# Packed attention and a GELU feed-forward on one core: a new table of priorities for the kernel's planner, with other lengths of the first transfers and a smaller margin on landings

## The chip, the core and the metric

The kernel runs on one core of a Trainium2 chip. The core has five engines with an instruction queue of their own: PE (TensorE, matrix products), ACT (ScalarE), DVE (VectorE), POOL (GpSimd) and SP (SyncE), which here only issues transfers (DMAs) between the chip's main memory and the core's memory. Each engine works its queue off in order and waits on semaphores for the others. The metric is the device time of one execution in microseconds (us), given as the median of several runs.

## The reference: what is computed

```
s  = softmax(p @ k^T / 8) @ v            # p: 32 packed queries a head; k, v: 576 x 64
a  = softmax(q @ s^T / 8) @ s            # q: 576 x 64; 8 batches x 8 heads
x  = a, heads side by side               # 4608 x 512
h  = x @ w_in                            # 512 x 2048
g  = 0.5 * h * (1 + erf(h / sqrt(2)))
out = g @ w_out                          # 2048 x 512, float32
```

## The kernel before, in words

The program is unrolled: Python code walks through all of the work once and emits one instruction stream for each engine. Batches are taken in pairs (four pairs, `NP`), and the hidden width of 2048 in four blocks of 512 (`NF`), which gives 16 units `u` of 8 steps. A step is one tile h (L1140 and L1149 on PE, with the packed product s @ w_in as a weight, `wp`, made by L1045 or L1084), then gelu on ACT (L1172), a rounded copy on ACT (L1179) and the rest by subtraction on DVE (L1181), which together are g, and then 12 matmuls of g with w_out (L1202 to L1204, name o). A pair's remainder of 64 rows a batch goes through POOL (L1192, L1193) and the o_edge matmuls. The two attention products of the first pair stand in the head of the program, in chunks of four heads: load, transposes on PE (L468 for k and q, L515 for p), scores (L591, L543), softmax on ACT and DVE, transposes of the weights (L667), the product with v (L707) and its transpose (L722). For the later pairs they are mixed into the steps of the pair before. The weights arrive as 64-bit words and are decoded (L980, L981 on ACT, L987 to L993 on DVE, L1007 to L1021 on POOL), kept in main memory once (L1026) and loaded again in later pairs (L948).

What stands where in each engine's queue is decided by a planner inside the kernel, the class `Order`. It holds a clock of its own, gives each operation an engine, a cost and a priority (`step`; the smallest goes first), and issues an operation as soon as its inputs, its buffers and its engine are free by that clock. The chip doesn't follow the clock, only the order that comes out of it. Four things in it matter here.

- Priorities come from the tables `FIRST` (the first pair), `SECOND` and `LATER` (the others), `LEAD` (weights), and `PATIENCE` and `STEADY` (how much later an operation may be and still go ahead of one that doesn't suit the engine at the moment).
- A transfer lands by the clock after an issue time, the bytes of its cost over 390 KB a microsecond, and a latency. For all that are issued after 1.5 us (`DMA_EARLY`) a margin `DMA_SLACK` is put on top.
- Where PE has nothing that is ready by the clock, and the first output matmul hasn't been issued, the planner emits a **filler**, a matmul on a constant tile `still` (L1122), of 0.11 us by its clock. In the profile and the order a PSUM tile that fillers used keeps the name idle, so `idle<-still` are the fillers, and `idle<-ident,k` is a transpose that took such a tile.
- Up to eight transfers are under way by the clock; SP issues them all.

```
done = self.under_way[-1] + (DMA_SLACK if self.now > DMA_EARLY else 0.0)
...
if engine == PE and self.idle and self.idle():
    self.free[PE] = self.now + self.clock(self.now, IDLE, True)
```

## Time and profile before

| | before |
|---|---|
| median of 3 runs | 729.41 us (729.28 to 729.71) |
| the profiled execution | 729.62 us |
| its span, first to last instruction | 727.8 us |
| matmuls on PE | 5594, of which 202 are fillers |
| moved by DMA | 106.8 MB |

Times in the profile are microseconds from the span's start. A row of a group gives the line, the engine, the operation with its output and inputs, how often it stands there, its busy time with the mean of one in ns, and the idle time of the engine before it with what ended it. A row of a timeline gives start, duration, line and operation, and in brackets the idle time before it. Matmuls overlap: PE's place is read from the distance of starts, not from the duration of one. A row of the DMA view gives the transfer, its size and the time from issue to landing.

### The profile page before, as it was taken

The numbers are of one execution on the slowest core, as the hardware profiler recorded it, in microseconds if no ns is written. First come the engines' busy times: TensorE is split into PE (matmuls) and PEld (weight loads), VectorE is DVE, ScalarE is ACT, GpSimd is POOL, SyncE is SP. The second block draws the span as 40 slices with busy tenths as digits, with TensorE's granted clock in tenths as the row PEclk, the third lists the DMA queues.
The fourth block names the chain that finished last, engine by engine and source line by source line (L and its number), as shares of the span: only waits on it lengthen the run. The fifth ranks groups of instructions, "written<-read, shape, count | busy, mean of one in ns | idle before, by whom it ended". The sixth has DMA issues, their size and how long they took to land.

```text
span 727.8 us, 13835 instructions
## 1 busy us (share of the span) xinstructions
PE 722.8 (99%) x5594; PEld 595.3 (82%) x5594; DVE 395.1 (54%) x608; ACT 347.3 (48%) x591; POOL 157.5 (22%) x331
## 2 busy tenths in 40 slices
PE   9999999999999999999999999999999999999998
PEld 7777787787878887887788887877887888888887
DVE  5898767888488334334687332444578321424322
ACT  4667775686365533553263343626254243324221
POOL 2554564644310100010111101101011101111110
PEclk9999999999999999999999999999999999999999
DMA  9959669697537967084723968053833603020122
GB/s 331 402 196 178 213 219 192 208 236 194 181 88 128 206 177 149 1 214 92 171 76 117 202 149 204 11 181 57 133 116 116 217 30 145 30 91 26 41 75 73
DMA packets 155135, 106.80 MB, mean 147 GB/s; under 512 B 123200, under 2 KB 129600, under 8 KB 155072
## 3 DMA queue, kind: packets, MB, share of 16 engines
q1 hardware_dynamic: 155072, 105.93, 56.1%
q8 instruction: 44, 0.72, 0.4%
q14 instruction: 19, 0.16, 0.1%
HBM read 83.89 MB, written 22.02 MB: 146 GB/s over the span
## 4 chain that ended last, share of the span: by engine, by line
PE 99%; ACT 0%; DVE 0%; issue 0%; ACTq 0%
PE h L1149 27%; PE o L1202 17%; PE o L1204 16%; PE o L1203 16%; PE wps L1084 4%; PE idle L1122 3%; PE s L543 2%; PE o_edge L1202 2%; PE o_edge L1204 2%; PE o_edge L1203 2%; PE pp L707 1%; PE h L1140 1%; PE e1Tm L655 1%; PE idle L707 1%; PE km L468 1%; PE qm L468 0%
## 5 line engine op out<-in xcount | busy, mean ns | idle before, releaser
L1149 PEld LDWEIGHTS h<-a2T,wp 128*128 128x128 f32 x1488 | 207.7, 188 | 9.0 <-ACT graw L1172 1.0
L1149 PE MATMUL h<-a2T,wp 128*128 128x288 f32 x1488 | 214.3, 295 | 0.6 <-ACT graw L1172 0.6
L1181 DVE TENSOR_TENSOR g<-graw,g 128x512 fp32r<-128x512 f32 x128 | 92.9, 726 | 208.5 <-ACT g L1179 198.7
L1172 ACT ACTIVATE graw<-h 128x576 f32<-128x576 f32 x127 | 82.3, 652 | 257.7 <-PE h L1149 201.6
L1202 PE MATMUL o<-w,g 128*128 128x512 f32 x508 | 204.8, 403 | 0.0
L1204 PE MATMUL o<-w,g 128*128 128x512 f32 x508 | 198.9, 392 | 0.0
L1203 PE MATMUL o<-w,g 128*128 128x512 f32 x508 | 198.8, 391 | 0.0
L1192 POOL CAST t<-graw 128x64 fp32r<-128x64 f32 x128 | 38.1, 298 | 495.2 <-ACT graw L1172 447.2
L1202 PEld LDWEIGHTS o<-w,g 128*128 128x128 f32 x508 | 95.4, 188 | 35.2 <-issue 16.8
L1204 PEld LDWEIGHTS o<-w,g 128*128 128x128 f32 x508 | 95.3, 188 | 21.5
L1203 PEld LDWEIGHTS o<-w,g 128*128 128x128 f32 x508 | 95.5, 188 | 15.4
L1179 ACT CAST g<-graw 128x512 fp32r<-128x512 f32 x128 | 79.6, 622 | 9.0 <-PE o L1204 6.4
L1288 DVE TENSOR_TENSOR acc<-o,acc 128x512 f32<-128x512 f32 x96 | 64.0, 685 | 33.6 <-PE o L1204 33.5
L1193 POOL TENSOR_TENSOR t<-graw,t 128x64 fp32r<-128x64 f32 x128 | 45.7, 357 | 10.2
L1096 DVE TENSOR_TENSOR wp<-wps,wp 128x1024 fp32r<-128x1024 f32 x30 | 35.3, 1218 | 13.7 <-ACT wp L1095 13.6
L1095 ACT CAST wp<-wps 128x1024 fp32r<-128x1024 f32 x30 | 29.0, 1018 | 15.2 <-PE wps L1084 15.2
L1084 PE MATMUL wps<-w,pp 64*32 64x512 f32 x480 | 29.2, 595 | 0.0
L1122 PE MATMUL idle<-still 128*128 128x256 bf16 x202 | 27.7, 286 | 1.1 <-DVE still L396 1.1
L993 DVE SCALAR_TENSOR_TENSOR wt<-wraw,wt 128x512 int32<-128x512 int32 x32 | 26.1, 814 | 0.6
L1015 POOL TENSOR_TENSOR wt<-wt 128x512 int32<-128x512 int32 x16 | 21.3, 1332 | 21.5 <-DVE wt L993 15.9
L1202 PE MATMUL o_edge<-w,t 128*128 128x512 f32 (+1 forms) x68 | 25.8, 379 | 0.0
L1122 PEld LDWEIGHTS <-still 128*128 128x128 bf16 x202 | 19.8, 102 | 7.3 <-issue 3.3
(138 smaller groups left out, 670.1 us busy)
## 6 DMA issues: line engine op xcount, KB each, us to landing
w<-ws SPq DMA_DIRECT2D x72, 512.0 KB, 5.2
ws<-w SPq DMA_DIRECT2D x24, 512.0 KB, 3.6
wraw<-in_moe_w_in_dram SPq DMA_DIRECT2D x16, 512.0 KB, 5.1
wraw<-in_moe_w_out_dram SPq DMA_DIRECT2D x16, 512.0 KB, 4.4
k<-in_k_dram SPq DMA_DIRECT2D x48, 144.0 KB, 4.8
q<-in_q_dram SPq DMA_DIRECT2D x48, 144.0 KB, 5.5
out_dram<-acc SPq DMA_DIRECT2D x26, 256.0 KB, 2.1
v<-in_v_dram SPq DMA_DIRECT2D x12, 512.0 KB, 4.4
```

The lines of the kernel that those rows point to most:

```text
L1084: nc.tensor.matmul(t[r0:r0 + 32, hh], lhsT=pp[b][rows, hh, r0:r0 + 32], rhs=wi[u, hh][rows, g], start=True, stop=True)
L1122: nc.tensor.matmul(bank(t)[:, :256], lhsT=still[:, :P], rhs=still, start=True, stop=True)
L1149: nc.tensor.matmul(t[:, half, :HALF], lhsT=w[:, wpart, ch, fc], rhs=a2T[b, ch][:, apart, half * HALF:(half + 1) * HALF], start=ch == 0 and ...
L1172: lambda raw: nc.scalar.activation(raw.rearrange("p (a n) -> p a n", a=2), t[:, :, :HALF], AF.Gelu),
L1179: g = yield Op(ACT, 0.52, lead, lambda g: nc.scalar.copy(g[:, 0], main), [(gts, f"g_{n}")])
L1181: DVE, 0.6, lead, lambda: nc.vector.tensor_tensor(g[:, 1], main, g[:, 0].bitcast(F32), ALU.subtract),
L1192: nc.gpsimd.tensor_copy(dst[:, 0], side)
L1193: nc.gpsimd.tensor_tensor(dst[:, 1], side, dst[:, 0].bitcast(F32), ALU.subtract)
L1202: nc.tensor.matmul(t, lhsT=g[0], rhs=w[:, 0], start=first, stop=False)
L1203: nc.tensor.matmul(t, lhsT=g[0], rhs=w[:, 1], start=False, stop=False)
L1204: nc.tensor.matmul(t, lhsT=g[1], rhs=w[:, 0], start=False, stop=last)
L1288: yield Op(DVE, 0.6, n, lambda: nc.vector.tensor_tensor(a, x, a, ALU.add))
```

## The change

Only numbers are changed. The margin on landings, `DMA_SLACK`, goes from 2.0 to 0.8 us. The sizes from which the planner works out the length of the first pair's transfers and of the weights' are smaller. And all entries of the tables of priorities are new; among them one chunk instead of two has its softmax subtraction and multiplication on POOL (`gpsimd`), the four copies of the first packed products are all on ACT (`copy`), one chunk's scores use another PSUM ring (`banks`), and one set of k's transposes is evacuated by ACT instead of DVE (`turn`).

```diff
-DMA_SLACK, DMA_EARLY = 2.0, 1.5
+DMA_SLACK, DMA_EARLY = 0.8, 1.5
...
-    "p": (-549.25, -438.34),
-    "k": (-613.55, -468.03, -440.86, -350.31),
+    "p": (-1320.01, -453.87),
+    "k": (-1227.69, -1055.77, -668.22, -531.18),
...
-    "gpsimd": (1, 2),
-    "copy": ("DVE", "ACT", "DVE", "ACT"),
-    "banks": (True, True, False, True),
-    "turn": {"k": ("ACT", "DVE", "DVE", "DVE"), "q": ("DVE", "ACT", "ACT", "ACT")},
+    "gpsimd": (1,),
+    "copy": ("ACT", "ACT", "ACT", "ACT"),
+    "banks": (True, True, True, False),
+    "turn": {"k": ("ACT", "DVE", "ACT", "DVE"), "q": ("DVE", "ACT", "ACT", "ACT")},
...
-        cost, fn = ((4, 1800e3, 1.1), blocks) if bt.b >= 2 else ((1, 650e3), ninths) if name == "k" else ((1, 620e3), rows)
+        cost, fn = ((4, 1800e3, 1.1), blocks) if bt.b >= 2 else ((1, 575e3), ninths) if name == "k" else ((1, 570e3), rows)
...
-        cost, fn = ((1, 650e3), ninths) if s.b < 2 else ((2, 900e3, 0.6), fn)
+        cost, fn = ((1, 610e3), ninths) if s.b < 2 else ((2, 900e3, 0.6), fn)
...
-        raw = yield Op(DMA, (1, 590e3 if i < 2 else 530e3), load_step, fetch, [(raws, f"wraw_{n}")])
+        raw = yield Op(DMA, (1, 530e3 if i < 2 else 510e3), load_step, fetch, [(raws, f"wraw_{n}")])
```

What it does to the queues is shown at three places. First SP's queue at the start of the program (names carry the batch and the chunk, then a number of the buffer). Before:

```order
L429 DMA k_0_0_84<-in_k_dram 128x2x576
L974 DMA wraw_0_0_1_86<-in_moe_w_in_dram 128x2x512
L509 DMA p_0_90<-in_p_dram 128x2x64 x2
L974 DMA wraw_0_1_0_97<-in_moe_w_in_dram 128x2x512
L970 DMA wraw_0_2_0_101<-in_moe_w_out_dram 128x1024
L429 DMA k_0_1_106<-in_k_dram 128x2x576
L426 DMA q_0_0_110<-in_q_dram 128x1152
```

and now:

```order
L509 DMA p_0_84<-in_p_dram 128x2x64 x2
L970 DMA wraw_0_2_0_89<-in_moe_w_out_dram 128x1024
L429 DMA k_0_0_93<-in_k_dram 128x2x576
L429 DMA k_0_1_97<-in_k_dram 128x2x576
L974 DMA wraw_0_0_1_101<-in_moe_w_in_dram 128x2x512
L429 DMA k_1_0_106<-in_k_dram 128x2x576
L974 DMA wraw_0_1_0_110<-in_moe_w_in_dram 128x2x512
```

p is now first, k third and fourth with a weight of w_out ahead of them, and q, which was seventh, comes fourteenth.

Second, PE's queue up to the first transposes of k. Before, 18 fillers stand ahead of these rows, 16 behind:

```order
L1122 LDWEIGHTS still_72
L1122 MATMUL idle_88<-still_72 128x256
L468 MATMUL idle_88<-ident_71,k_0_0_84 128x128 x3
L468 MATMUL km_0_0_1_126<-ident_71,k_0_0_84 128x128 x3
L468 MATMUL km_0_0_2_131<-ident_71,k_0_0_84 128x128 x3
L515 MATMUL pTm_0_144<-ident_71,p_0_90 128x128 x2
```

and now, after 12 fillers, with 18 of them between p and k (the line of three dots):

```order
L1122 MATMUL idle_87<-still_72 128x256
L515 MATMUL idle_87<-ident_71,p_0_84 128x128 x2
L1122 LDWEIGHTS still_72
L1122 MATMUL idle_116<-still_72 128x256
...
L468 MATMUL idle_116<-ident_71,k_0_0_93 128x128 x3
L468 MATMUL km_0_0_1_157<-ident_71,k_0_0_93 128x128 x3
L468 MATMUL km_0_0_2_162<-ident_71,k_0_0_93 128x128 x3
```

The transposes of p went from behind those of the first k to ahead of them: they come after 12 fillers now, and came after 18 fillers and nine transposes.

Third, ACT's queue around the softmax of batch 2 in the second pair (e2 are its weights, h_29 and graw_29 a step's hidden tile and its gelu, ppTm the transposed packed product of batch 3). Before:

```order
L803 ACT_TABLE_LOAD
L803 ACTIVATE e2_2_0_2629<-e2_2_0_2629 128x18x32
L803 ACTIVATE e2_2_1_2630<-e2_2_1_2630 128x18x32
L715 ACTIVATE pn_3_1_2742<-pp_3_1_2677,st_3_1_1873 128x128
L1172 ACT_TABLE_LOAD
L1172 ACTIVATE graw_29_2752<-h_29_2727 128x576
L726 COPY pp_3_2513<-ppTm_3_1_2746 128x128
```

and now:

```order
L715 ACTIVATE pn_3_1_2708<-pp_3_1_2675,st_3_1_1524 128x128
L803 ACT_TABLE_LOAD
L803 ACTIVATE e2_2_0_2624<-e2_2_0_2624 128x18x32
L726 COPY pp_3_2433<-ppTm_3_1_2714 128x128
L803 ACTIVATE e2_2_1_2625<-e2_2_1_2625 128x18x32
L1172 ACT_TABLE_LOAD
L1172 ACTIVATE graw_29_2751<-h_29_2720 128x576
```

The copy of ppTm went from behind the gelu to ahead of the switch of tables, between the two exponentials. Over the whole program the counts of every kind of matmul are the same but for the fillers, 193 instead of 202.

## The prediction

> **What bounds the kernel now.** I read the page first, for who is busy and what the last chain consists of.

> ```profile
> PE 722.8 (99%) x5594; PEld 595.3 (82%) x5594; DVE 395.1 (54%) x608; ACT 347.3 (48%) x591; POOL 157.5 (22%) x331
> PE 99%; ACT 0%; DVE 0%; issue 0%; ACTq 0%
> ...
> L1122 PE MATMUL idle<-still 128*128 128x256 bf16 x202 | 27.7, 286 | 1.1 <-DVE still L396 1.1
> ```

> TensorE (PE) is 99% of the chain that ended last, so the time is the length of its instruction stream plus the holes in it. Part of that stream is not work: 202 matmuls on a constant tile, the fillers of L1122, which the planner puts where it expects PE to wait. Next, where PE really waits:

> ```profile
> PE idle L1122 <- DVE still L396: 1.1, 1, 1.1
> PE h L1149 <- ACT graw L1172: 0.6, 1, 0.6
> ```

> These two rows are all of PE's waits in the run: 1.1 us before its first instruction and 0.6 once. So PE is held by no transfer anywhere. Where it would have waited, a filler stands instead, and a filler that is in the program runs whether its time is needed or not. A smaller margin can therefore gain only through **fewer fillers**, fewer changes of PE's mode, or another course of the 0.6. The windows say the same for the late part (the columns after the window are the length, then PE's busy time and its instructions):

> ```profile
> 550.00:650.00 100.00, 100.00 (x592) 85.08 (x585) 37.87 (x54) 36.89 (x58) 12.42 (x39) 1.00 0.29 96
> 650.00:728.00 78.00, 74.56 (x432) 64.19 (x430) 24.58 (x37) 19.75 (x30) 8.79 (x30) 1.00 0.20 70
> ```

> The last row leaves 3.4 us without PE, the last store. PE's last 12 rows are the same instructions in the same order in the changed program, so I take that as unchanged.

> **The change part by part.** *Fillers.* The order of the changed program holds 193 fillers against 202; every other kind of matmul has the same count. A filler's price, once PE runs at full rate, from the PE timeline:

> ```profile
> 1.05 4.02 PE L1122 MATMUL idle<-still 128*128 128x256 bf16 x18 [1.05 <-DVE still L396]
> 4.87 0.85 PE L468 MATMUL idle<-ident,k 128*128 128x128 f32 x3
> ...
> 6.80 0.53 PE L515 MATMUL pTm<-ident,p 128*128 128x128 f32 x2
> 7.16 1.91 PE L1122 MATMUL idle<-still 128*128 128x256 bf16 x16
> ...
> 9.68 4.32 PE L1122 MATMUL idle<-still 128*128 128x256 bf16 x38
> 13.84 0.49 PE L468 MATMUL idle<-ident,k 128*128 128x128 f32 x3
> ```

> From 9.68 to 13.84, 38 fillers: 0.109 us each. Nine fewer: **-0.98 us**. (The first 18 took 4.87 - 1.05 = 3.82 us, 0.212 each: until about 7.0 PE ran at half rate. If that stretch keeps its length, what stands in it doesn't matter to the sum.)

> *Changes of mode.* The small tiled matmuls (L543, L591, L667, L707, L1045, L1084) stand in runs between the full ones. A run costs something at both ends:

> ```profile
> 81.59 0.39 PE L1202 MATMUL o<-w,g 128*128 128x512 f32 x1
> 81.81 0.39 PE L1203 MATMUL o<-w,g 128*128 128x512 f32 x1
> 82.04 0.39 PE L1204 MATMUL o<-w,g 128*128 128x512 f32 x1
> 82.36 1.95 PE L1084 MATMUL wps<-w,pp 64*32 64x512 f32 x32
> 84.24 0.50 PE L1202 MATMUL o<-w,g 128*128 128x512 f32 x1
> 84.57 0.40 PE L1203 MATMUL o<-w,g 128*128 128x512 f32 x1
> ```

> Start to start a full matmul takes 0.22 to 0.23; into the run it is 0.32, and the first one behind it 0.33: 0.1 each. Counted in the order there are 52 such runs before and 55 now: 3 x 0.2 = **+0.6 us** (from 0.3, if one end is hidden by weight loads, to 0.6).

> *The first transfers.* Fillers are only saved if the transfers are there. This is the one place where PE arrives earlier than the rows of before let me confirm: the program now starts with p. Issues from the queue's timeline, times to landing from the DMA view of four windows:

> ```profile
> 0.74 0.43 SPq L429 DMA_DIRECT2D k<-in_k_dram  x1
> 1.23 0.46 SPq L974 DMA_DIRECT2D wraw<-in_moe_w_in_dram  x1
> 1.73 0.97 SPq L509 DMA_DIRECT2D p<-in_p_dram  x2
> 2.75 0.47 SPq L974 DMA_DIRECT2D wraw<-in_moe_w_in_dram  x1
> 3.26 0.47 SPq L970 DMA_DIRECT2D wraw<-in_moe_w_out_dram  x1
> 3.77 0.43 SPq L429 DMA_DIRECT2D k<-in_k_dram  x1
> ```

> ```profile
> k<-in_k_dram SPq DMA_DIRECT2D x1, 576.0 KB, 3.9
> ```

> ```profile
> wraw<-in_moe_w_in_dram SPq DMA_DIRECT2D x1, 512.0 KB, 4.9
> ```

> ```profile
> p<-in_p_dram SPq DMA_DIRECT2D x2, 64.0 KB, 4.6
> ```

> ```profile
> k<-in_k_dram SPq DMA_DIRECT2D x1, 576.0 KB, 7.2
> wraw<-in_moe_w_in_dram SPq DMA_DIRECT2D x1, 512.0 KB, 5.5
> wraw<-in_moe_w_out_dram SPq DMA_DIRECT2D x1, 512.0 KB, 6.2
> ```

> So k lands at 4.64, w at 6.13, the two p about 6.6 (1.98 + 4.6), later weights at 8.25 and 9.46, k at 10.97: one after the other, 1.2 us for 512 KB, 1.5 for 576 KB, 0.5 for both p. With p first: 4.64 - 1.5 + 0.5 = 3.6, and since its second half is issued 0.5 us after the first, up to 4.2; I take 3.8. PE gets to p after 12 fillers at half rate, 1.05 + 12 x 0.212 = 3.6. The wait is **+0.2 us** (0 to 0.6).

> Next is k, third in the queue: 3.8 + 1.2 + 1.5 = 6.5. PE is there after 18 more fillers, 13 at half rate to 7.0 and 5 at 0.109: 7.6. The second k lands at 8.0 and is wanted at 7.6 + 9 x 0.109 + 4 x 0.109 = 9.0. In before the second k landed at 10.97 and was used at 13.84. The margin falls from 2.9 us to about 1.0, and stays above nothing: no cost.

> *The 0.6.* The one wait on ScalarE (ACT) is a table switch in front of a gelu:

> ```profile
> 205.83 1.28 ACT L1172 ACT_TABLE_LOAD   x1 [1.23 <-PE h L1149]
> 207.12 0.65 ACT L1172 ACTIVATE graw<-h 128x576 f32<-128x576 f32 x1
> ```

> ```profile
> 207.83 1.46 PE L1149 MATMUL h<-a2T,wp 128*128 128x288 f32 x9 [0.57 <-ACT graw L1172]
> ```

> The next h needed the PSUM tile that this gelu frees. In the changed order the small product in front (ppTm) stands ahead of h_29 and its copy ahead of the switch, so the next h finds the other tile free: I take **-0.6 us** (0 if a like wait comes up elsewhere). The two sub-steps of softmax that move from POOL to DVE, and the copies that move to ACT, lie in the head, where neither engine held PE, and I cost them at nothing; if that cover were gone, a 0.7 us operation of DVE would show in full.

> Sum: -0.98 + 0.6 + 0.2 - 0.6 = **-0.8 us**. The profiled execution took 729.62 (span 727.8), so 728.8; the median of the three runs is 729.41, 0.2 lower, so for a median **728.7 us**, -0.1%. A measurement of this kernel tells about 0.2% (1.46 us) from no change, so this is "the same".

> **The rivals.** *Slower, by waits on later loads.* The margin falls by 1.2 us on all later loads too, and the loads of k and q for later batches go to DVE, which also makes g:

> ```profile
> DVE kT L457 <- DMA k<-in_k_dram: 1.6, 1, 1.6
> ```

> ```profile
> 89.13 1.74 PE L1149 MATMUL h<-a2T,wp 128*128 128x288 f32 x12
> 90.71 0.39 PE L1202 MATMUL o<-w,g 128*128 128x512 f32 x1
> ...
> 93.46 0.83 PE L1149 MATMUL h<-a2T,wp 128*128 128x288 f32 x5
> ```

> ```profile
> L1181 DVE TENSOR_TENSOR g<-graw,g 128x512 fp32r<-128x512 f32 x128 | 92.9, 726 | 208.5 <-ACT g L1179 198.7
> L1172 ACT ACTIVATE graw<-h 128x576 f32<-128x576 f32 x127 | 82.3, 652 | 257.7 <-PE h L1149 201.6
> ...
> L1179 ACT CAST g<-graw 128x512 fp32r<-128x512 f32 x128 | 79.6, 622 | 9.0 <-PE o L1204 6.4
> ```

> PE does a step of o (2.75 us) and the next h (1.58) before it wants a new g, 4.3 us; gelu, cast and subtraction take 0.65 + 0.62 + 0.73 = 2.0. So DVE may stand 2 us or so before PE feels it: that is the point from which this decides. The 1.6 of before cost PE nothing. With 1.2 more it would be 2.8, 0.8 over. Three such places give 2.4: 731.1. Against it: only one wait of DVE on these loads in the whole run, and the two rows show ACT and DVE waiting for PE some 200 us, not the other way round.

> *Slower, by a late full rate.* PE ran at half rate from 1.05 to 7.0, busy all that time. If the hole at p makes the six microseconds count anew from 3.8, half rate lasts to 9.8, and 2.8 us more at half rate lose 1.4: 730.1, or 730.5 with the longest wait at p. For it: the rows can't tell how full a stretch must be. [...]

> *Faster.* No wait at p (-0.2), runs at 0.3 (-0.3) and a few hidden tenths in PE's stream gone: 728.7 - 1.0 = 727.7.

> *The change doesn't do what it says*: margins on landings that nobody waits for bring nothing by themselves. That is the forecast itself, near nothing, with the fillers as what is left.

> **How the numbers follow.** Forecast 728.7 with its own range of 728.0 to 729.9: 0.61. Waits on later loads, 731.1: 0.15. Late full rate, 730.1 to 730.5, which is inside "the same" unless waits add to it: 0.12, a third of it over the bound. Faster, 727.7: 0.12. So faster by over 0.2% (under 727.95) 0.12, slower by over 0.2% (above 730.87) 0.15 + 0.04 = 0.19, the same 0.69. The range leaves out the ends of the two outer cases: 727.7 to 731.1.

> **What would show it.** Right: the fillers' row with x193; PE's first p at 3.7 to 4.0 with a wait of a few tenths; the 109 ns filler from about 7 us on; the first o (57.49 before) within 1.5 us of where it was, no PE wait on a transfer behind 10 us, and the ACT graw wait gone. Wrong: a first full-rate filler only near 10 us; PE rows that wait on L1181 or L1172 by more than 1 us in sum; DVE waits on k or q over 2 us; or holes in the head that ACT or DVE end, for then the order of the head, not its transfers, was too tight.

## The result, and the profile after

| | before | after |
|---|---|---|
| median | 729.48 us (729.28 to 729.71, 4 runs) | 738.60 us (738.33 to 739.83, 4 runs) |
| ratio | | 1.0128, 95% interval 1.0111 to 1.0146 |
| span of the profiled execution | 727.8 us | 736.6 us |

The change makes the kernel 9.1 us slower. The forecast was 0.7 us faster, and its range ended at 731.1. The page of after still shows a kernel that PE bounds:

```profile
PE 727.9 (99%) x5585; PEld 593.0 (81%) x5585; DVE 393.1 (53%) x606; ACT 349.7 (47%) x596; POOL 153.7 (21%) x328
PE 97%; ACT 1%; DMA 1%; issue 0%; SPq 0%; DVE 0%; ACTq 0%
...
L1122 PE MATMUL idle<-still 128*128 128x256 bf16 x193 | 27.0, 290 | 1.1 <-DVE still L396 1.1
```

The nine fillers are gone, yet PE is busy 5 us longer than the 722.8 of before with nine matmuls less, and ACT and DMA have a share of the chain that they didn't have. PE's waits in after, all of them (the columns are the sum, how often, and the longest):

```profile
PE e1Tm L655 <- ACT graw L1172: 1.6, 2, 0.8
PE pp L707 <- issue: 1.3, 1, 1.3
PE pp L707 <- ACT e1T L659: 1.1, 2, 0.6
PE idle L1122 <- DVE still L396: 1.1, 1, 1.1
PE idle L468 <- DMA k<-in_k_dram: 0.3, 1, 0.3
```

Only the fourth was there before. The others sum to 4.3 us, and the wait of 0.6 that before had is gone, so they leave some 5 us of the loss without a wait: those are the busy time. Which matmuls take it shows in the groups by line (busy time, then the mean of one in ns), before:

```profile
L1149 PE MATMUL h<-a2T,wp 128*128 128x288 f32 x1488 | 214.3, 295 | 0.6 <-ACT graw L1172 0.6
L1204 PE MATMUL o<-w,g 128*128 128x512 f32 x508 | 198.9, 392 | 0.0
L1203 PE MATMUL o<-w,g 128*128 128x512 f32 x508 | 198.8, 391 | 0.0
```

and after:

```profile
L1149 PE MATMUL h<-a2T,wp 128*128 128x288 f32 x1488 | 213.1, 294 | 0.0
L1203 PE MATMUL o<-w,g 128*128 128x512 f32 x508 | 201.0, 396 | 0.0
L1204 PE MATMUL o<-w,g 128*128 128x512 f32 x508 | 200.9, 396 | 0.0
```

The output matmuls, unchanged in count and shape, are 4 to 5 ns longer each; the hidden ones 1 ns shorter. Because matmuls overlap, the distance of starts says it better: averaged over the successive rows of L1202 to L1204 that stand side by side in the trace (without some 60 distances of over 300 ns, nearly all at the first one behind a run of small matmuls), it is 229.5 ns before and 233.2 ns after; in stretches of 50 us it is 228.6 to 231.1 before and 232.9 to 233.4 after. Between rows of L1149 it is 132.9 and 131.9. With 1524 output matmuls, 204 for the edges (from 215.6 to 218.3 ns) and 1488 hidden ones that is 5.6 + 0.6 - 1.5 = 4.7 us, an estimate from these distances.

### The profile page after: what moved, and what is told of

It reads as the page before. It is cut to its first block, busy times and chain, and to the rows that moved or that the text cites. A ratio compares the mean times of both kernels' runs of the same rounds, so it can differ in the third digit from the quotient of the medians.

```text
span 736.6 us, 13802 instructions
## 1 busy us (share of the span) xinstructions
PE 727.9 (99%) x5585; PEld 593.0 (81%) x5585; DVE 393.1 (53%) x606; ACT 349.7 (47%) x596; POOL 153.7 (21%) x328
## 4 chain that ended last, share of the span: by engine, by line
PE 97%; ACT 1%; DMA 1%; issue 0%; SPq 0%; DVE 0%; ACTq 0%
PE h L1149 27%; PE o L1202 17%; PE o L1203 16%; PE o L1204 16%; PE wps L1084 4%; PE idle L1122 3%; PE s L543 2%; PE o_edge L1202 2%; PE o_edge L1204 2%; PE o_edge L1203 2%; PE pp L707 2%; PE h L1140 1%; DMA k<-in_k_dram 1%; ACT L1172 1%; PE e1Tm L655 1%; PE idle L707 0%
## 5 line engine op out<-in xcount | busy, mean ns | idle before, releaser
L1149 PEld LDWEIGHTS h<-a2T,wp 128*128 128x128 f32 x1488 | 207.1, 188 | 8.8
L1172 ACT ACTIVATE graw<-h 128x576 f32<-128x576 f32 x128 | 83.2, 651 | 274.6 <-PE h L1149 232.0
L1149 PE MATMUL h<-a2T,wp 128*128 128x288 f32 x1488 | 213.1, 294 | 0.0
L1181 DVE TENSOR_TENSOR g<-graw,g 128x512 fp32r<-128x512 f32 x128 | 94.7, 741 | 218.1 <-ACT g L1179 211.2
L1202 PE MATMUL o<-w,g 128*128 128x512 f32 x508 | 206.8, 407 | 0.0
L1203 PE MATMUL o<-w,g 128*128 128x512 f32 x508 | 201.0, 396 | 0.0
L1204 PE MATMUL o<-w,g 128*128 128x512 f32 x508 | 200.9, 396 | 0.0
L1192 POOL CAST t<-graw 128x64 fp32r<-128x64 f32 x128 | 39.6, 309 | 505.0 <-ACT graw L1172 464.0
L1202 PEld LDWEIGHTS o<-w,g 128*128 128x128 f32 x508 | 95.6, 188 | 38.3 <-issue 19.5
L1204 PEld LDWEIGHTS o<-w,g 128*128 128x128 f32 x508 | 95.7, 188 | 22.7
L1203 PEld LDWEIGHTS o<-w,g 128*128 128x128 f32 x508 | 95.8, 189 | 16.8
L1179 ACT CAST g<-graw 128x512 fp32r<-128x512 f32 x128 | 79.6, 622 | 7.6 <-PE o L1204 4.5
L1084 PE MATMUL wps<-w,pp 64*32 64x512 f32 x480 | 29.2, 595 | 0.0
L1122 PE MATMUL idle<-still 128*128 128x256 bf16 x193 | 27.0, 290 | 1.1 <-DVE still L396 1.1
L1007 POOL TENSOR_TENSOR w<-wt 128x512 int32<-128x512 int32 x16 | 22.6, 1411 | 19.8 <-DVE wt L993 11.4
L1202 PE MATMUL o_edge<-w,t 128*128 128x512 f32 (+1 forms) x68 | 26.2, 385 | 0.0
L1204 PE MATMUL o_edge<-w,t 128*128 128x512 f32 (+1 forms) x68 | 26.0, 382 | 0.0
## 6 DMA issues: line engine op xcount, KB each, us to landing
w<-ws SPq DMA_DIRECT2D x72, 512.0 KB, 5.4
ws<-w SPq DMA_DIRECT2D x24, 512.0 KB, 5.0
wraw<-in_moe_w_out_dram SPq DMA_DIRECT2D x16, 512.0 KB, 4.6
wraw<-in_moe_w_in_dram SPq DMA_DIRECT2D x16, 512.0 KB, 4.8
v<-in_v_dram SPq DMA_DIRECT2D x12, 512.0 KB, 4.7
```

The costliest lines, as they stand in the source:

```text
L1084: nc.tensor.matmul(t[r0:r0 + 32, hh], lhsT=pp[b][rows, hh, r0:r0 + 32], rhs=wi[u, hh][rows, g], start=True, stop=True)
L1122: nc.tensor.matmul(bank(t)[:, :256], lhsT=still[:, :P], rhs=still, start=True, stop=True)
L1149: nc.tensor.matmul(t[:, half, :HALF], lhsT=w[:, wpart, ch, fc], rhs=a2T[b, ch][:, apart, half * HALF:(half + 1) * HALF], start=ch == 0 and ...
L1172: lambda raw: nc.scalar.activation(raw.rearrange("p (a n) -> p a n", a=2), t[:, :, :HALF], AF.Gelu),
L1179: g = yield Op(ACT, 0.52, lead, lambda g: nc.scalar.copy(g[:, 0], main), [(gts, f"g_{n}")])
L1181: DVE, 0.6, lead, lambda: nc.vector.tensor_tensor(g[:, 1], main, g[:, 0].bitcast(F32), ALU.subtract),
```

## The experiments

The ratios compare each kernel with runs of the kernel before on the same chip. The gains against after are differences of medians from different chips; the medians of before on these lie between 729.47 and 729.69 us, so a gain is uncertain by a few tenths. Three questions were open: why the output matmuls are slower, what the four waits on ACT are, and what the wait called "issue" is, which has no releaser in the profile.

### Where the tiles stand

The memory of the core is laid out by the program: a group of tiles gets its address when its first tile is taken. Another order of work takes them in another order, so most tiles moved. In the allocation of the two programs the w tiles (the moving operand of the output matmuls) stand from 155616 on before and from 135584 after, the g tiles (the stationary one) from 189920 and 196320. To move the addresses without touching the order, the first tile of each group is taken ahead of all work, in the other program's order; that adds no instruction (on the kernel after; the list is one line there):

```diff
     accs = ring("acc", 9, [P, DM])
+    [r.next(r.tag + "_0") for r in (wis, mxs, mx2s, xraws, a2ts, praws, wraws, xts, wts, wps,
+     vraws, pts, sts, sms, e1ts, wos, pns, pps, graws, gts, t4s, a2raws, accs)]
```

> The changed kernel, its order of instructions untouched, with every tile group at the SBUF address that it has in the kernel before. Theory A (placement): about 4 us of the 9.1 us lost come from output matmuls that start every 233.2 ns in place of 229.5 ns, and this pace is set by where the tiles stand in SBUF, which the new order moved; expects 733.5 to 735.5 us and a pace near 229.5 ns at L1202 to L1204. Theory B (the order itself, or the chip's state on that run, sets the pace): expects 738 to 739.5 us and 233 ns. Both expect the stalls of PE at 37, 263, 325, 437 and 499 us to stay.

> The kernel before, its order of instructions untouched, with every tile group at the SBUF address that it has in the changed kernel. Theory A (placement): the output matmuls fall back to 233 ns from start to start; expects 733 to 735 us. Theory B (order or chip state): expects 729.0 to 730.0 us and 229.5 ns.

The changed kernel at the old addresses: 734.01 us (ratio to before 1.0073, 1.0048 to 1.0098), 4.6 us faster than after, 229.4 ns from start to start, all its waits where they were. The kernel before at the new addresses: 735.07 us (1.0077, 1.0062 to 1.0092), 5.6 us slower than before and just above the 735 us that was expected, 233.2 ns, no new wait. One line of each, in that order:

```profile
L1204 PE MATMUL o<-w,g 128*128 128x512 f32 x501 | 196.2, 392 | 0.0
```

```profile
L1204 PE MATMUL o<-w,g 128*128 128x512 f32 x501 | 198.1, 395 | 0.0
```

(Here 501, because the first tile of w carries another name.) So the pace goes with the addresses, whatever the order. The next three narrow down which. The first gives graw, g, t4 and a2 their old addresses and leaves the rest; the second puts 64 bytes ahead of the w tiles and 448 behind them; the third 192 ahead of g:

```diff
+    pads = [ring(f"pad{i}", 1, [P, n]) for i, n in enumerate((16, 112,))]
+    [r.next(r.tag + "_0") for r in (..., xts, pads[0], wos, pads[1], sts, ...)]
```

> The changed kernel with only graw, g, t4 and a2 at the addresses of before (g from 196320 to 189920); w, wp and a2T stay where the change put them. If the place of the stationary operand g sets the pace of the output matmuls: 733.5 to 735.5 us and 229.5 ns from start to start. If the place of the moving operand w (or of a2T and wp) sets it: 738 to 739.5 us and 233 ns.

> The changed kernel with the w tiles 64 bytes further (135584 to 135648, which leaves the same remainder of 128, 96, as in the kernel before) and everything behind them 512 bytes further. If the remainder of w's address by 128 or less sets the pace: 733.5 to 735.5 us and 229.5 ns. If g's place or w's place in larger blocks sets it: 738 to 739.5 us and 233 ns.

> The changed kernel with only g 192 bytes further (196320 to 196512; acc behind it too), w and t4 untouched. Rule from the runs of matmuls alone (fast where the addresses of w and g have the same remainder by 256): the remainder of w minus g goes from 192 to 0, the pace of the output matmuls from 233 to 229.5 ns, 733.6 to 734.6 us. Rival (w's own remainder by 128 is what counts, as one could read the run with w moved): 738 to 739.5 us and 233 ns.

| run | w | g | (w - g) mod 256 | start to start | median, us |
|---|---|---|---|---|---|
| before | 155616 | 189920 | 0 | 229.5 ns | 729.5 |
| after | 135584 | 196320 | 192 | 233.2 ns | 738.6 |
| after, old addresses | 155616 | 189920 | 0 | 229.4 ns | 734.01 |
| before, new addresses | 135584 | 196320 | 192 | 233.2 ns | 735.07 |
| after, old g, graw, t4, a2 | 135584 | 189920 | 192 | 233.2 ns | 739.06 |
| after, w 64 bytes on | 135648 | 196832 | 0 | 229.4 ns | 733.57 |
| after, g 192 bytes on | 135584 | 196512 | 0 | 229.0 ns | 733.45 |

The last row moved g (and acc, which stands behind it), and the one above it moved w against g, by 64 bytes modulo 256; both win 5 us. The run with w moved came in as expected, but for another reason than the expectation gave: it was not w's own remainder, which the last row left as it was in after. The fifth gave g its old address and won nothing, for the difference stayed at 192. It is not the place of either tile that decides but the **distance of the two, modulo 256 bytes**. The full course of it comes from a kernel that runs only such matmuls, 60 in a row in the pattern of L1202 to L1204, at 32 places of w and g:

```diff
+    [nc.tensor.matmul(**x) for x in seq(0, 0)]
+    [nc.tensor.matmul(**x) for x in seq(32, 0)]
...
```

The first of these lines is L40, with w and g at the same remainder; the second is L41, with w 32 bytes further.

> None of the kernel's work: only runs of 60 matmuls in the pattern of L1202 to L1204, with nothing else running, 16 runs with w at each multiple of 32 bytes within 512, then 16 with g at each. Theory A, if the place alone within 512 bytes acts: some runs near 226 to 230 ns and others near 233 ns from start to start, following the offset of w, of g, or both. If the pace comes from where tiles stand in larger blocks or from what other engines write and read at the same time: all runs the same within 1 ns.

Its groups by line, costliest first; L40, L41, L42, L44 and L46 have w moved by 0, 32, 64, 128 and 192 bytes:

```profile
L44 PE MATMUL o<-w,g 128*128 128x512 f32 x60 | 14.7, 395 | 0.0
...
L41 PE MATMUL o<-w,g 128*128 128x512 f32 x60 | 14.7, 395 | 0.0
L46 PE MATMUL o<-w,g 128*128 128x512 f32 x60 | 14.7, 396 | 0.0
...
L42 PE MATMUL o<-w,g 128*128 128x512 f32 x60 | 14.4, 391 | 0.0
...
L40 PE MATMUL o<-w,g 128*128 128x512 f32 x60 | 14.2, 389 | 0.0
```

L40 and L42, with w at the same remainder as g and 64 bytes further, are the short ones. By the distance of starts, averaged over each run of 60:

| (w - g) mod 256 | 0 | 32 | 64 | 96 | 128 | 160 | 192 | 224 |
|---|---|---|---|---|---|---|---|---|
| w moved, ns | 226.6 | 233.5 | 228.6 | 234.3 | 233.3 | 234.4 | 233.6 | 232.6 |
| the same difference, g moved, ns | 228.4 | 233.6 | 228.7 | 232.9 | 232.6 | 233.6 | 233.6 | 232.9 |

The second 256 bytes repeat the first to 0.1 ns, but for difference 0, which gives 226.6 or 226.7 in three runs and 228.4 in two. Nothing else runs here (no DMA packet from 36.3 to 37.6 us, nothing on ACT from 258 to 266), so this is PE with itself. Its weight loads run beside its matmuls: in after a matmul of L1202 starts at 101.05 us, the weight load of the next one, L1203, at 101.06, for 0.19 us, and that matmul at 101.28; over the run PEld is busy for 593.0 us and PE for 727.9, in a span of 736.6. So it reads the moving operand and the next weights at the same time. That these two readings meet in memory would fit a dependence on their distance, which makes 7 ns in 227 here, but no run takes one of them away, so this is argued and not shown, and where the two would meet no run shows.

The same for the hidden matmuls, whose two halves stand 1152 bytes apart, 128 modulo 256:

> None of the kernel's work: runs of the hidden matmuls (128x288, pattern of L1149) with a2T at each multiple of 32 bytes from wp, with the two halves 1152 bytes apart as in the kernel or 1280, then 12 hidden and 12 output matmuls in turn with other distances of a2T from wp and of g from w. If the rule found for the output matmuls (fast where the remainders of the two addresses by 256 are equal) holds for these too: 1280 bytes at distance 0 is the fastest, by 3 to 6 ns from start to start, and 1152 lies between. If not: all alike within 1 ns.

This expectation failed: 131.7 to 133.3 ns for all distances, 131.7 or 133.3 for halves 1280 bytes apart as well, a spread of 1.6 ns where 3 to 6 were expected (a first run, 134.4, is left out). The shorter matmul hardly cares, and there was nothing to win in a2T's place. The output matmuls, mixed with hidden ones in the same kernel, keep their rule: 227.3 to 228.4 ns at difference 0 in five of six mixed runs (the sixth is broken by pauses and isn't counted), 233.3 to 233.5 with g moved by 64 bytes, 228.8 by 192.

### The waits on ACT

At all four places ACT loads its other table in front of a gelu, after some exponentials of the next pair's softmax. One of them, from the timelines of ACT and then of PE:

```profile
260.72 0.19 ACT L634 ACTIVATION_READ_ACCUMULATOR e<-e,mx 128x1 f32 x1
262.37 1.28 ACT L1172 ACT_TABLE_LOAD   x1 [1.46 <-PE h L1149]
263.66 0.65 ACT L1172 ACTIVATE graw<-h 128x576 f32<-128x576 f32 x1
```

```profile
263.30 0.27 PE L656 MATMUL e1Tm<-ident,e 128*64 128x128 f32 x1
264.36 0.75 PE L655 MATMUL e1Tm<-ident,e 128*128 128x128 f32 x4 [0.79 <-ACT graw L1172]
```

ACT is idle for 1.46 us and then loads for 1.28: the load stands behind the wait for h, although it needs nothing of h: moved ahead, in the run below, it is done 1.4 us before h arrives. At 325 and 499 us the idle time ahead of the load is 2.94 us. At 437 us it is only 0.36, and there the load ahead of the exponentials, at 432.59, stands behind 2.55 us of idle time as well; the load ahead of the gelu is this row:

```profile
435.87 1.28 ACT L1172 ACT_TABLE_LOAD   x1 [0.36 <-PE h L1149]
```

The planner charges a switch from the time when the engine came free, `begin = max(begin, self.free[engine] + TABLE_SWITCH)`, so by its clock an idle ACT has the load behind it when h arrives. A small activation of the coming table, ahead of the one that waits, lets the load run in the idle time:

```diff
-        op.fn(*tiles)
+        self.load_table(op.table) if op.table and op.table != self.table else None; op.fn(*tiles)
...
+    order.load_table = lambda table: nc.scalar.activation(nothing, still[:, :1], AF.Gelu if table == "gelu" else AF.Exp)
```

The first attempt had the call a few lines lower, behind `op.fn`, so that the small activation stood behind the gelu and the load where it had been:

> The changed kernel with one small activation of the coming table put ahead of each activation that changes ACT's table, so that the 1.28 us table load runs when ACT reaches it and not after the wait for the hidden matmuls. Theory C (exposed table loads): the four stalls of PE at 263, 325, 437 and 499 us, 0.6 to 0.9 us each, 2.9 us in sum, go; expects 735.0 to 736.5 us and no PE wait over 0.3 us at those places. Rival D (the stalls come from the order of the chains, and the load only stands there by chance): expects 738 to 739.5 us, with PE still waiting at those places for PSUM or for the copy of e1T.

> The kernel before with the same small activation ahead of each change of ACT's table. Theory C: the one wait of 0.57 us at 207.8 us goes and nothing else changes, 728.6 to 729.3 us. Rival D: 729.3 to 730.0 us, the 22 added activations costing nothing or a little.

739.07 us (1.013, 1.0115 to 1.0145) and 729.69 us (1.0005, 0.9996 to 1.0015), all waits on ACT in place. These say nothing on the theory, only that 22 small activations cost nothing to be seen. (The profiled execution of the second, 731.23 us, also has waits of 0.9 us on p and of 0.9 called "issue", which comes up again below.) With the call at the right place:

> The changed kernel with the small activation truly ahead of each activation that changes ACT's table (in the run before it had come to stand behind it, and the load stayed at the gelu). Theory C (exposed table loads): the load runs during ACT's wait for the hidden matmuls; the four stalls of PE at 263, 325, 437 and 499 us, 2.9 us in sum, go; expects 735.0 to 736.8 us. Rival D: 738 to 739.5 us.

> The kernel before with the small activation truly ahead of each change of ACT's table: the term of -0.6 us in the prediction, taken alone. Theory C (the gelu of a changed table costs what of its load stands behind the hidden matmuls): the wait of 0.57 us at 207.8 us goes, 728.7 to 729.3 us, and its stall at 206.9 us is not in the trace. Rival: the added activations or another wait take it back, 729.4 to 730.0 us.

The changed kernel: 735.13 us (1.0074, 1.0059 to 1.0089), 3.5 us faster than after. The same place:

```profile
259.89 1.28 ACT L1127 ACT_TABLE_LOAD   x1
261.18 0.20 ACT L1127 ACTIVATE nothing<-still 128x1 f32<-128x1 bf16 x1
262.61 0.65 ACT L1172 ACTIVATE graw<-h 128x576 f32<-128x576 f32 x1 [1.23 <-PE h L1149]
```

The load ends at 261.17, h arrives at 262.61, and no PE wait on ACT is left. The kernel before: 728.78 us (0.9989, 0.9980 to 0.9998); its wait of 0.6 is gone, and only PE's first row is left among its waits. Theory C holds on both, with 3.5 us on the one and 0.8 on the other. That is somewhat more than PE's waits, 2.7 and 0.6; where the rest comes from is open.

### The wait called "issue"

It stands in the middle of a run of small matmuls of one instruction group, which wait for nothing:

```profile
36.31 1.09 PE L707 MATMUL pp<-v,e1T 64*32 64x64 f32 x63
38.72 0.26 PE L707 MATMUL pp<-v,e1T 64*32 64x64 f32 x4 [1.32 <-issue]
```

The view of DMA queues shows, beside the data, a queue of instructions. From 36.3 to 37.6 us (packets, MB, share of the 16 engines):

```profile
q1 hardware_dynamic: 158, 0.47, 94.5%
q8 instruction: 1, 0.02, 5.3%
```

q8 moves 44 packets of 16384 bytes in the run, 720,896 bytes, and the trace holds 11293 instructions of PE: 63.8 bytes for each, so a packet is some 256 instructions. Counted in the trace, the stall comes after 1217 of them, and a packet starts at 36.4 and ends at 37.5, 1.2 us before PE goes on. The block of 256 ahead of the stall lasted from 33.0 to 37.2, 4.2 us; it is full of small matmuls. In after the packets start 2.4, 3.1, 2.4 and 3.4 us behind the edges of their blocks at 12.5, 20.8, 27.6 and 33.0 us, while data moves at 390 to 415 GB/s. They start 1.1 and 0.6 us behind the next two edges and 0.2 us ahead of the third, at 133 to 280 GB/s. The theory: PE used up a block faster than the next one came through the busy DMA engines. If the packet that ends 1.2 us before PE goes on carries the block that PE waited for, as the theory has it, it started only when PE was inside the block before, 3.4 us behind the edge at 33.0; how many blocks PE can hold no run shows. To move the edges without moving the work, the first fillers are issued as two halves of 128 columns:

```diff
+    t4, gs, acc, halves = {}, {}, {}, []
...
-                nc.tensor.matmul(bank(t)[:, :256], lhsT=still[:, :P], rhs=still, start=True, stop=True)
+                halves.append(len(halves) < 28); [nc.tensor.matmul(bank(t)[:, c], lhsT=still[:, :P], rhs=still[:, c],
+                    start=True, stop=True) for c in ((slice(0, P), slice(P, 256)) if halves[-1] else (slice(0, 256),))]
```

> The changed kernel with the first 28 fillers each issued as two of 128 columns in place of one of 256: the same PE time within 0.2 us, 56 instructions more. Theory E (PE waits at 37.2 us for its own instructions: a block of 256 is fetched over the same busy DMA engines, and the block before it, full of small matmuls, is used up in 4.2 us): the edges of the blocks move to places where each block lasts over 5.1 us, the stall of 1.5 us goes, 736.8 to 737.6 us. Rival F (the stall belongs to the matmuls at that place, say to the landing of v or to a clock step): it stays at the same matmul, 738.3 to 739.3 us.

> The kernel before with the first 44 fillers each issued as two of 128 columns. Theory E: 88 instructions more move the edges of the blocks so that one block is used up in 3.5 us and a stall of 1.4 to 2.3 us comes up in the run of small matmuls behind 28.5 us, where there was none; 730.5 to 731.8 us. Rival F: no stall, 729.3 to 730.0 us.

The changed kernel: 737.53 us (1.0104, 1.0089 to 1.0119), 1.1 us faster than after (737.1 to 737.7 against 738.3 to 739.8); the "issue" wait is gone from PE's list, and its small matmuls run through:

```profile
36.76 1.30 PE L707 MATMUL pp<-v,e1T 64*32 64x64 f32 x65
37.85 0.43 PE L543 MATMUL s<-qT,pp 64*32 64x288 f32 x1
```

65 of them start between 36.76 and 37.85, 17 ns apart.

In the kernel before, a stall comes up where there was none, after 961 instructions, exactly 256 ahead of the 1217:

```profile
28.57 1.26 PE L707 MATMUL idle<-v,e1T 64*32 64x64 f32 x71
30.26 0.21 PE L707 MATMUL idle<-v,e1T 64*32 64x64 f32 x1 [0.44 <-issue]
```

The place is as expected, the size less than half of it (a gap of 0.65 us between two starts), and the time not: 729.69 us (0.9999, 0.9990 to 1.0009). PE is 0.68 us late at 30.3 us and level with before again at 40.8; the small matmuls of before around 33 and behind 38.86 us, at the old edges, run that much slower than here. So theory E holds for the stall, and a stall moved is not always time won.

The other traces agree. In all nine profiled executions of the whole kernel with an "issue" wait in PE's list, it stands after 961 or after 1217 instructions, whatever work is there, and PE goes on 1.2 to 1.5 us after the end of the packet. The run of before with the small activation behind the gelu is one of them, with a stall after 961 that the profiled execution of before itself doesn't have. What stays argued is that the data transfers make the packets late, for no run changes the data queue alone.

### The three together

> The changed kernel with three edits together: w 64 bytes further (as in the run with w moved), the small activation ahead of each change of ACT's table, and the first 28 fillers each issued as two of 128 columns, which makes PE's instruction stream 56 instructions longer ahead of the stall at 37 us. If the three causes are separate and together the whole loss: 738.6 - 5.0 - 3.5 - 1.4 = 728.7 us (728 to 730). If they overlap or something else is lost too: over 730.5 us.

728.99 us (0.9987, 0.9978 to 0.9997): 9.6 us faster than after, where the three alone sum to 5.0 + 3.5 + 1.1 = 9.6. PE's waits in this kernel:

```profile
PE idle L1122 <- DVE still L396: 1.1, 1, 1.1
PE idle L468 <- DMA xraw<-in_k_dram: 0.5, 1, 0.5
PE pTm L515 <- DMA p<-in_p_dram: 0.2, 1, 0.2
```

The causes are separate and make up the whole loss, within the few tenths by which such gains are uncertain. This and the kernel before with its table loads ahead (728.78 us) are the two versions that beat both kernels, by 0.1%, less than the bound of 0.2% that the prediction set. Both have the table loads ahead, and they are alike within 0.2 us: the new tables of priorities, freed of what they lost by accident, are worth no more than the old ones.

## Why the prediction was wrong

**The step that failed most: what a matmul costs.** "Every other kind of matmul has the same count" was taken to mean the same time. The prediction reads 0.22 to 0.23 us from start to start as the price of a full matmul and never asks what sets it. The order moved the addresses, the distance of w and g went from 0 to 192 modulo 256, and 3.7 ns on each output matmul, less what the hidden ones gave back, made 4.7 us by the trace and 4.6 to 5.6 by experiment. No rival named it.

**The -0.6 for the table load.** The mechanism was seen, a load in front of a gelu that PE waits for, and it was booked as a gain because the one place of before was mended by the new order. The clause "0 if a like wait comes up elsewhere" was the right question, bounded wrongly: four such waits came up, 1.6 + 1.1 us by PE's rows; the first two alone are the sign of being wrong that the prediction set at 1 us on L1172. The term should have been 2.7 in place of -0.6; taken out by itself the mechanism measures 3.5 on after and 0.8 on before. The planner's line that treats a load as hidden was open to read, and with it every place where a switch follows an idle time of ACT is suspect.

**The head.** Right: 193 fillers, and p's wait within 0 to 0.6. The rows:

```profile
1.05 2.74 PE L1122 MATMUL idle<-still 128*128 128x256 bf16 x12 [1.05 <-DVE still L396]
3.66 0.66 PE L515 MATMUL idle<-ident,p 128*128 128x128 f32 x2
4.12 3.11 PE L1122 MATMUL idle<-still 128*128 128x256 bf16 x18
7.52 0.55 PE L468 MATMUL idle<-ident,k 128*128 128x128 f32 x3 [0.29 <-DMA k<-in_k_dram]
```

p came in time, less than 0.1 us late in this execution and up to 0.7 in the other runs of the changed order. The rival of a late full rate is out: 18 fillers in 3.1 us are 0.173 each, between the half-rate 0.212 and the 0.109, so full rate came before 7 us, no later than in before, whose fillers are 0.109 apart from 7.16 on; by their starts the fillers are 0.213 apart until 6.0 us and 0.109 from 6.2. k was late by 0.3 where the sum had it 1.1 us early: the weight and k took some 3.8 us behind p (from 3.7 to 7.5), not the 2.7 that the rows of before gave them; the weight of w_out landed at 5.9 (issued at 1.73, landed 4.2 later). The first output matmul came at 59.81, 2.3 us later than before and outside the 1.5 that the prediction allowed. That sign was a poor one: 24 of the hidden matmuls of L1140 stand ahead of it now and 16 stood there before, and the eight more, 0.243 us apart, are 1.9 us of work that only moved forward. With the fillers halved, and the stall on instructions gone, it came at 58.92, 0.9 us earlier. That stall was in no term: PE's own instructions were not counted among the transfers.

**The rivals.** Slower by waits on later loads was right in sign and wrong in mechanism: DVE's waits on k fell from 1.6 us to 1.3 in sum, and no PE wait on a transfer stands behind 10 us. "Holes in the head that ACT or DVE end" did not come either; the holes that ACT ends stand at 263 to 499 us, in the later pairs.

**What was right, and what agrees by chance.** The counts were right, and most of the small terms were near. Fillers, changes of mode and p were put at -0.98 + 0.6 + 0.2 = -0.2 us and the table load at -0.6, together 728.7 (729.41 less 0.8 is 728.6; the prediction rounded up); the mended kernel takes 728.99. That the two numbers meet is in part luck. The mended kernel's gain over before on the same chip, 0.7 us, is no more than the table loads alone are worth in before, 0.8 us. Against the kernel before with its table loads ahead, 728.78 us on another chip, what is left for the first three terms is +0.2 us, or +0.7 by the spans of the profiled executions (727.4 and 726.7 us). By the distance of starts, the fillers with the transposes of k, q and p take some 0.9 us less in the mended kernel than in before if the waits for transfers are left out (predicted 0.98); the waits for k and p are 0.7 us (predicted 0.2); and the runs of small matmuls, 55 and no longer 52, with what they cost at both ends, take about 1 us more (predicted 0.6).

## What to carry to other kernels

Where a change reorders a program that takes its buffers in order of use, compare the addresses of the operands that the bounding engine reads as well as its instructions: for fp32r matmuls of 512 columns here, keep moving and stationary tiles at equal remainders modulo 256 bytes (229.0 to 229.5 ns from start to start against 233.2 at a difference of 192), which cost 192 bytes of padding in the run with g moved. Let a table load stand ahead of the wait, with a small activation that needs nothing (3.5 us on after, 0.8 on before). And compare two profiles by the time per instruction of the bounding engine, not only by its waits: about half of this loss, 4.7 of 9.1 us, showed in no wait.
